# A fused block-sparse attention and squared-ReLU MLP kernel: mask and one-hot rows built another way, weights staged through eight buffers

## The chip, the cores and the metric

The kernel runs on one core of a Trainium2 chip. The metric is device time in microseconds (us) of one execution. It is the median over several executions; before the change three executions took 393.23, 394.69 and 397.41 us, so the median is 394.69 us. A core has five engines that run their own instruction streams and wait for one another through semaphores: PE (matrix products; PEld is its weight load), DVE (VectorE), ACT (ScalarE), POOL (GpSimd) and SP (SyncE, which in this kernel issues the DMA transfers).

## The reference

Four batches, eight heads, 768 positions, head size 64. Each query block of 32 positions may look at neighbouring blocks, at the first and last block, and at three sampled blocks. The attention output then goes through a two-layer MLP with a squared ReLU.

```
scores = scale * q @ k.T
mask   = |blk_i - blk_j| <= 1  or  either block is first or last  or  blk_j in sampled_blocks[blk_i]
attn   = softmax(where(mask, scores, -1e9))
x      = (attn @ v), heads joined          # 3072 tokens x 512
g      = relu(x @ w_in) ** 2               # w_in  512 x 2048
out    = g @ w_out                         # w_out 2048 x 512
```

Inputs and output are float32, the block list is 64-bit integers (the kernel reads the low 32-bit half). Matrix products run on bfloat16.

## The kernel before, in words

**Attention.** Heads go in pairs; a pair of one batch is a unit `u`, and there are 16 units, four to a batch. A unit has nine steps `s` (three stretches of 256 queries by three pairs of key chunks), 144 steps in all. `scores(s)` makes four products K·Q into the PSUM tile `ps`, and ACT takes the exponential into `pT`. `values(s - 2)` multiplies by V into `po`, of which there is one buffer, and every third step DVE copies `po` out into `et`.

**The mask.** It is not added by an engine: it rides in the products. The operands have extra rows under (QA, KA) or above (QB, KB) the 64 rows of data. In K these rows are a one-hot code of the key's block (24 rows); in Q they hold, for each query, 0 or a large negative number by block. The position order inside a tile is permuted: column n·128+p stands for position p·6+n. Before, DVE builds two 24-column tables (`oh`, `t2`), on all partitions, and `spread` (L146) writes each out to 24x768 in the permuted order, four tensors for each of two alternating buffer sets, eight copies in all.

**Loading and preparation.** `load(u)` issues three transfers (`qs`, `ks`, `vs`) on SP; `cast_qk` and `cast_v` turn them into bfloat16 on DVE; `transp` has PE transpose them and DVE copy the result into the data rows.

**After a unit.** `sums_out` sends the softmax sums from `et` into a small tile `st`, `recip` takes the reciprocal on DVE and sends it to DRAM (`rd`), `spread_recip` reads it back broadcast over 64 partitions (`rt`), and `normalize` multiplies `et` by it into `xT`.

**Weights.** There are 16 pieces of 512 KB. `w_load(i)` brings a piece into a float32 stage `wst`, `w_cast(i)` casts it on DVE into `w_in_sb` or `w_out_sb`.

**MLP.** For each batch, `h_atom` makes four products into `ph`, DVE takes the ReLU (`r`), POOL squares it (`g`), and `y_atom` makes four products into `py`. The pieces are spread evenly over 36 attention steps by the loop at the end, which starts a batch's MLP `LAG` steps after its last attention step; what is left of the last batch runs alone at the end.

**Order.** Each engine runs its instructions in the order in which the code emits them; nothing is reordered. `at(s, f)` puts `f` behind `scores(s)` and ahead of the MLP pieces and `values(s - 2)` of that step. Hence a DVE instruction that waits for a transfer also holds everything behind it on DVE, and an SP transfer that waits holds all later transfers. Each transfer also takes one of eight semaphores in turn, so a transfer waits until the one eight places ahead of it has landed.

Of the kernel before, what the change touches and what calls it, by code (L numbers as in the profile page):

```python
# [24 lines left out]
def kernel(  # L25
# [15 lines left out]
    nc = tc.nc  # L41
    B, H, S, D = q.shape
    block = 32
    nb = S // block
# [5 lines left out]
    NCH = S // P  # L50
# [37 lines left out]

    sb_i = consts.tile([P, nb * n_rand * 2], I32, name="sb_i")
    sb32 = sampled_blocks.bitcast(I32)  # L90
    nc.sync.dma_start(
        out=sb_i, in_=sb32.rearrange("q r -> (q r)").unsqueeze(0).broadcast_to([P, nb * n_rand * 2]))
    load(0)
    load(1)


    identb = consts.tile([P, P], BF, name="identb")
    make_identity(nc, identb)


    kbi = consts.tile([P, 1], I32, name="kbi")
    nc.gpsimd.iota(kbi[:64, :], pattern=[[0, 1]], base=0, channel_multiplier=1)
    nc.gpsimd.iota(kbi[64:, :], pattern=[[0, 1]], base=0, channel_multiplier=1)
    qbi = consts.tile([P, nb], I32, name="qbi")
    nc.gpsimd.iota(qbi, pattern=[[1, nb]], base=0, channel_multiplier=0)

    QA, QB, KA, KB, VA, VB = [], [], [], [], [], []
    NPB = 2
    for i in range(NPB):
# [7 lines left out]
    kbf = consts.tile([P, 1], F32, name="kbf")  # L117
    qbf = consts.tile([P, nb], F32, name="qbf")
    sbf = consts.tile([P, nb, n_rand], F32, name="sbf")
    eq = consts.tile([P, nb, n_rand], F32, name="eq")  # L120
    hit = consts.tile([P, nb], F32, name="hit")
    t1 = consts.tile([P, nb], F32, name="t1")
    t2 = consts.tile([P, nb], F32, name="t2")
    oh = consts.tile([P, nb], F32, name="oh")
    edge = consts.tile([P, 2], F32, name="edge")
    V = nc.vector
    V.tensor_copy(out=kbf, in_=kbi)
    V.tensor_copy(out=qbf, in_=qbi)

    V.tensor_scalar(out=oh, in0=qbf, scalar1=kbf, scalar2=None, op0=AOP.is_equal)  # L130
    V.tensor_scalar(out=t1, in0=qbf, scalar1=kbf, scalar2=None, op0=AOP.subtract)
    V.tensor_scalar(out=t2, in0=t1, scalar1=-1.0, scalar2=None, op0=AOP.is_ge)
    V.scalar_tensor_tensor(out=t1, in0=t1, scalar=1.0, in1=t2, op0=AOP.is_le, op1=AOP.mult)
    V.tensor_scalar(out=edge[:, 0:1], in0=kbf, scalar1=0.0, scalar2=None, op0=AOP.is_equal)
    V.tensor_scalar(out=edge[:, 1:2], in0=kbf, scalar1=float(nb - 1), scalar2=None, op0=AOP.is_equal)
    V.tensor_scalar(out=t1, in0=t1, scalar1=edge[:, 0:1], scalar2=edge[:, 1:2], op0=AOP.max, op1=AOP.max)
    V.memset(t1[:, 0:1], 1.0)
    V.memset(t1[:, nb - 1:nb], 1.0)
    sb_lo = sb_i.rearrange("p (q r two) -> p q r two", r=n_rand, two=2)[:, :, :, 0]
    V.tensor_copy(out=sbf, in_=sb_lo)  # L140
    V.tensor_scalar(out=eq, in0=sbf, scalar1=kbf, scalar2=None, op0=AOP.is_equal)
    V.tensor_reduce(out=hit, in_=eq, axis=AX.X, op=AOP.max)
    V.tensor_max(out=t2, in0=hit, in1=t1)
    V.tensor_scalar(out=t2, in0=t2, scalar1=-1.0, scalar2=-NEG, op0=AOP.add, op1=AOP.mult)

    def spread(dst, src, lo):  # L146

        V.tensor_copy(
            out=dst[lo:lo + nb, :].rearrange("k (n p) -> k p n", p=P),
            in_=src[lo:lo + nb, :].unsqueeze(2).broadcast_to([nb, nb, block]))  # L150

    G = nc.gpsimd
    for i in range(NPB):
        G.memset(QB[i][0:64, :], 0.0)
        G.memset(KB[i][0:64, :], 0.0)
        spread(KA[i], oh, 64)
        spread(KB[i], oh, 0)
        spread(QA[i], t2, 64)
        spread(QB[i], t2, 0)
        if i == 0:  # L160
            pass

    cast = {}

    def cast_qk(u):
        qs, ks, vs = raw[u]
        qc = work.tile([P, NCH, 2, D], BF, name="qc", tag="qc")
        kc = work.tile([P, NCH, 2, D], BF, name="kc", tag="kc")
        V.tensor_copy(out=qc, in_=qs.rearrange("p t n d -> p n t d"))  # L169
        V.tensor_copy(out=kc, in_=ks.rearrange("p t n d -> p n t d"))  # L170
        cast[u] = (qc, kc)

    def cast_v(u):
        vs = raw[u][2]
        i = u % NPB
        V.tensor_copy(out=VA[i][:, :, 0:D], in_=vs[:, 0])
        V.tensor_copy(out=VB[i][:, :, D:P], in_=vs[:, 1])

    def init_v(i):
        G.memset(VA[i][:, :, D:P], 0.0)  # L180
        G.memset(VA[i][:, :, D:D + 1], 1.0)
        G.memset(VB[i][:, :, 0:D], 0.0)
        G.memset(VB[i][:, :, 0:1], 1.0)

    def transp(u, which):
        src = cast[u][which]
        i = u % NPB
        A, Bt = (QA[i], QB[i]) if which == 0 else (KA[i], KB[i])
        pt = ps_h.tile([P, S], BF, name="pt", tag="h")
        for n in range(NCH):  # L190
            nc.tensor.transpose(pt[:, n * P:(n + 1) * P],  # L191
                                src[:, n, :, :].rearrange("p t d -> p (t d)"), identb)
        V.tensor_copy(out=A[0:D, :], in_=pt[0:D, :])  # L193
        V.tensor_copy(out=Bt[D:P, :], in_=pt[D:P, :])  # L194
# [86 lines left out]
    def recip(u):  # L281
        st = stile.pop(u)
        rc = work.tile([2 * SR, S // SR], F32, name="rc", tag="rc")
        V.reciprocal(out=rc, in_=st)  # L284
        rd = dram.tile([2, S], F32, name="rd", tag="rd")
        nc.sync.dma_start(out=rd.rearrange("t (a b) -> (t a) b", a=SR), in_=rc)
        rdram[u] = rd

    def spread_recip(u):
        rd = rdram.pop(u)  # L290
        rt = work.tile([P, S], F32, name="rt", tag="rt")
        nc.sync.dma_start(out=rt[0:D, :], in_=rd[0:1, :].broadcast_to([D, S]))
        nc.sync.dma_start(out=rt[D:P, :], in_=rd[1:2, :].broadcast_to([D, S]))
        rtile[u] = rt

    def normalize(u):
# [4 lines left out]
        V.tensor_mul(out=xT[b][0:D, a, :], in0=et[0:D, 0, :], in1=rt[0:D, :])  # L301
        V.tensor_mul(out=xT[b][D:P, a, :], in0=et[D:P, 1, :], in1=rt[D:P, :])  # L302
# [46 lines left out]
        return [z for _, _, z in sorted(both, key=lambda e: e[:2])]  # L349


    for i in range(NPB):
        init_v(i)
        if i == 0:
            cast_qk(0)
            cast_v(0)
    transp(0, 0)
    transp(0, 1)

    later = {}  # L360

    def at(s, f):
        later.setdefault(s, []).append(f)

    SPU = NQ * CP
    for u in range(NU):
        s0 = u * SPU
        if u + 2 < NU:
            at(s0 + 1, lambda u=u: load(u + 2))
# [68 lines left out]
```

## Time and profile before

| what | value |
|---|---|
| median of three executions | 394.69 us |
| the profiled execution, its own time | 392.2 us |
| its span, first to last instruction | 390.4 us |
| PE busy | 321.2 us (82%) |
| DVE busy | 238.2 us (61%) |
| ACT busy | 160.1 us (41%) |
| POOL busy | 113.8 us (29%) |
| moved by DMA | 40.49 MB, mean 104 GB/s |

The execution's own time is 1.8 us longer than the span. In the profile's rows, a line starts with the start time in us and the duration; in the stretch table each engine has its busy time; "PEclk" is the share of the full TensorE clock that was granted; a row of waits names the engine and line that waited, what it waited for, the total, the number and the longest. A DMA row on SP (SPq) is the issue of a transfer, not the transfer.

### The profile page before, as it was taken

Reading aid. Unit: us, or ns where it says so; the run is one execution under the profiler, and the core shown is the slowest. Engines: PE = TensorE matmul, PEld = TensorE weight load, DVE = VectorE, ACT = ScalarE, POOL = GpSimd, SP = SyncE. Lnnn points to the kernel's source line nnn. Section 1 sums busy time; section 2 is a strip of 40 time slices with the busy share of each in tenths; the row PEclk is TensorE's granted clock in tenths of the full one; section 3 lists DMA queues with packets and bytes.
Section 4 is the critical chain, followed back from the end, with each engine's and each line's share of the span. In section 5 each row is a group of like instructions: output and inputs, shape, how many; then the busy total and the mean of one; then the engine's idle time right before and its main releaser. Section 6 shows DMA issues by size and latency. Waiting matters only on the chain.

```text
span 390.4 us, 5784 instructions
## 1 busy us (share of the span) xinstructions
PE 321.2 (82%) x2215; PEld 217.7 (56%) x2240; DVE 238.2 (61%) x392; ACT 160.1 (41%) x169; POOL 113.8 (29%) x149
## 2 busy tenths in 40 slices
PE   0048627347889889999999999999999997999995
PEld 0037515235766666777667667666676663555542
DVE  7975625337677868677777667767665465444410
ACT  1027523236765545565554545554545521001011
POOL 5000000000004643233324343333433433666530
PEclk9999865688989999999999999999999999999999
DMA  7055356665550404421450155014111102000111
GB/s 234 15 160 191 110 156 229 208 202 177 164 161 19 146 19 146 128 93 41 151 188 31 40 152 190 31 53 156 49 60 37 41 30 95 29 27 28 55 54 54
DMA packets 23595, 40.49 MB, mean 104 GB/s; under 512 B 2960, under 2 KB 15376, under 8 KB 23568
## 3 DMA queue, kind: packets, MB, share of 16 engines
q1 hardware_dynamic: 23568, 40.13, 31.5%
q8 instruction: 17, 0.28, 0.3%
q14 instruction: 10, 0.08, 0.1%
HBM read 33.63 MB, written 6.39 MB: 102 GB/s over the span
## 4 chain that ended last, share of the span: by engine, by line
PE 62%; DVE 16%; DMA 14%; issue 3%; SPq 2%; ACT 1%; POOL 1%; DVEq 0%; ACTq 0%
PE py L325 19%; PE ph L310 17%; PE po L260 6%; PE po L262 6%; PE ps L244 6%; PE ps L242 6%; DMA st<-et 4%; DVE r L313 2%; DMA wst<-in_moe_w_in_dram 2%; DVE et L267 2%; PE pt L191 2%; DMA wst<-in_moe_w_out_dram 2%; DMA rd<-rc 2%; DMA sb_i<-in_sampled_blocks_dram 1%; DMA qs<-in_q_dram 1%
## 5 line engine op out<-in xcount | busy, mean ns | idle before, releaser
L246 ACT ACTIVATE pT<-ps 128x1024 bf16<-128x1024 f32 x144 | 145.8, 1023 | 161.8 <-PE ps L244 161.7
L315 POOL TENSOR_TENSOR g<-r 128x384 bf16<-128x384 f32 x128 | 108.0, 851 | 261.3 <-DVE r L313 261.3
L313 DVE TENSOR_SCALAR r<-ph 128x384 f32<-128x384 f32 x128 | 70.8, 556 | 71.1 <-PE ph L310 52.6
L310 PE MATMUL ph<-xT,w_in_sb 128*128 128x384 bf16 x512 | 100.9, 325 | 4.1 <-DVE r L313 3.4
L260 PE MATMUL po<-pT,VA 128*128 128x256 bf16 x288 | 75.5, 287 | 33.9 <-DVE et L267 33.9
L325 PE MATMUL py<-w_out_sb,g 128*128 128x512 bf16 x359 | 92.9, 379 | 3.1 <-ACT ys L329 1.4
L242 PE MATMUL ps<-QA,KA 88*128 88x256 bf16 x288 | 76.5, 288 | 1.4 <-DVE KA L193 1.2
L244 PE MATMUL ps<-QB,KB 128*128 128x256 bf16 x288 | 76.0, 286 | 0.3 <-DVE KB L194 0.3
L262 PE MATMUL po<-pT,VB 128*128 128x256 bf16 x288 | 75.7, 287 | 0.0
L310 PEld LDWEIGHTS <-w_in_sb 128*128 128x128 bf16 x512 | 49.5, 97 | 36.6 <-issue 3.8
L262 PEld LDWEIGHTS <-VB 128*128 128x128 bf16 x288 | 29.4, 102 | 48.5 <-issue 37.3
L325 PEld LDWEIGHTS <-g 128*128 128x128 bf16 x384 | 36.9, 97 | 35.0 <-issue 3.4
L329 ACT COPY ys<-py 128x512 f32<-128x512 f32 x24 | 14.0, 583 | 64.9 <-PE py L325 64.5
L267 DVE COPY et<-po 128x512 f32<-128x512 f32 x48 | 33.0, 688 | 11.4 <-PE po L262 10.9
L260 PEld LDWEIGHTS <-VA 128*128 128x128 bf16 x288 | 29.5, 103 | 11.8
L242 PEld LDWEIGHTS <-KA 88*128 88x128 bf16 x288 | 29.7, 103 | 6.7 <-DVE KA L193 1.4
L244 PEld LDWEIGHTS <-KB 128*128 128x128 bf16 x288 | 29.8, 103 | 6.2 <-issue 1.1
L191 PE MATMUL pt<-identb,qc 128*128 128x128 bf16 x96 | 8.6, 230 | 22.8 <-DVE qc L169 22.8
L284 DVE RECIPROCAL rc<-st 16x96 f32<-16x96 f32 x16 | 11.8, 737 | 17.2 <-DMA st<-et 17.2
L191 PEld LDWEIGHTS <-qc 128*128 128x128 bf16 x96 | 7.1, 103 | 23.3 <-DVE qc L169 22.8
L301 DVE TENSOR_TENSOR xT<-et,rt 64x768 bf16<-64x768 f32 x16 | 16.1, 1006 | 2.2 <-DMA rt<-rd 2.2
L302 DVE TENSOR_TENSOR xT<-et,rt 64x768 bf16<-64x768 f32 x16 | 15.3, 955 | 0.5
(48 smaller groups left out, 126.3 us busy)
## 6 DMA issues: line engine op xcount, KB each, us to landing
qs<-in_q_dram SPq DMA_DIRECT2D x16, 384.0 KB
ks<-in_k_dram SPq DMA_DIRECT2D x16, 384.0 KB
vs<-in_v_dram SPq DMA_DIRECT2D x16, 384.0 KB
rt<-rd SPq DMA_DIRECT2D x32, 192.0 KB
out_dram<-ys SPq DMA_DIRECT2D x24, 256.0 KB
wst<-in_moe_w_in_dram SPq DMA_DIRECT2D x8, 512.0 KB
wst<-in_moe_w_out_dram SPq DMA_DIRECT2D x8, 512.0 KB
st<-et SPq DMA_DIRECT2D x32, 3.0 KB
```

The source lines that it names most:

```text
L191: nc.tensor.transpose(pt[:, n * P:(n + 1) * P], src[:, n, :, :].rearrange("p t d -> p (t d)"), identb)
L242: nc.tensor.matmul(ps[:, c, 0, :], KA[i][0:64 + nb, ksl], QA[i][0:64 + nb, qsl], start=True, stop=True)
L244: nc.tensor.matmul(ps[:, c, 1, :], KB[i][:, ksl], QB[i][:, qsl], start=True, stop=True)
L246: nc.scalar.activation(out=pT, in_=ps, func=AF.Exp, scale=scale)
L260: nc.tensor.matmul(po[:, 0, :], VA[i][:, n, :], pT[:, c, 0, :], start=first, stop=last, skip_group_check=True)
L262: nc.tensor.matmul(po[:, 1, :], VB[i][:, n, :], pT[:, c, 1, :], start=False, stop=last, skip_group_check=True)
L267: V.tensor_copy(out=etile[u][:, :, qi * QW:(qi + 1) * QW], in_=po)
L301: V.tensor_mul(out=xT[b][0:D, a, :], in0=et[0:D, 0, :], in1=rt[0:D, :])
L310: nc.tensor.matmul(ph, w_in_sb[:, kc, f * P:(f + 1) * P], xT[b][:, kc, t * TW:(t + 1) * TW], start=(kc == 0), stop=(kc == KM - 1))
L313: V.tensor_scalar(out=r, in0=ph, scalar1=0.0, scalar2=None, op0=AOP.max)
L315: G.tensor_mul(out=g, in0=r, in1=r)
L325: nc.tensor.matmul(py, gtile[b, t, f][:, ts * P:(ts + 1) * P], w_out_sb[:, f, :], start=(f == 0), stop=(f == NF - 1))
```

## The change

1. **Mask and one-hot rows.** POOL makes the one-hot rows of K directly in the permuted order: DVE sets the 64x768 area to one, and two selects (`affine_select`) on POOL clear what lies outside the block. The table of masks is worked out by DVE on 24 partitions, in a PSUM tile `pm`, and goes as a 24x128 bfloat16 tile `bm` into two small products with the one-hot rows (`pb`); ACT copies the result into the rows of Q. The block list comes in as 24x6 integers, not broadcast to 128 partitions. Only the first buffer set is made in this way; the second is copied from it by four transfers on SP.
2. **Start.** `ks` of the first unit is issued by ACT; the first casts and transposes stand ahead of `init_v` and `cast_v`.
3. **Weights.** `wst` has eight buffers where it had two. `w_load(i)` stands at step 2+2i (before: 9+i) and `w_cast(i)` at 10+2i (before: 12+i).
4. **After a unit.** `recip` and `spread_recip` stand one step later, `normalize` two, and `LAG` is 12, not 10.

```diff
-    def load(u):
+    def load(u, eng):
...
-        nc.sync.dma_start(out=ks.rearrange("p t n d -> p t (n d)"), in_=kv[b, a])
+        eng.dma_start(out=ks.rearrange("p t n d -> p t (n d)"), in_=kv[b, a])
...
-    sb_i = consts.tile([P, nb * n_rand * 2], I32, name="sb_i")
...
+    sb_i = consts.tile([nb, n_rand * 2], I32, name="sb_i")
+    nc.sync.dma_start(out=sb_i, in_=sampled_blocks.bitcast(I32))
+    load(0, nc.scalar)
+    load(1, nc.sync)
...
+    G.iota(rel, pattern=[[1, nb]], base=0, channel_multiplier=-1, **small)
+    G.iota(col, pattern=[[1, nb]], base=0, channel_multiplier=0, **small)
+    G.iota(row, pattern=[[0, 1]], base=0, channel_multiplier=1, **small)
+    def one_hot(dst):
+        d3 = dst.rearrange("a (n p) -> a n p", p=P)
+        G.affine_select(out=d3, in_=d3, compare_op=AOP.is_ge, fill=0.0, base=0,
+                        pattern=[[1, NCH], [NCH, P]], channel_multiplier=-block)
+        G.affine_select(out=d3, in_=d3, compare_op=AOP.is_ge, fill=0.0, base=block - 1,
+                        pattern=[[-1, NCH], [-NCH, P]], channel_multiplier=block)
+    V.memset(KB[0][0:64, :], 1.0)
+    V.memset(KA[0][64:P, :], 1.0)
+    one_hot(KB[0][0:64, :])
+    identb = consts.tile([P, P], BF, name="identb")
+    make_identity(nc, identb)
+    one_hot(KA[0][64:P, :])
...
-    def spread(dst, src, lo):
-        V.tensor_copy(
-            out=dst[lo:lo + nb, :].rearrange("k (n p) -> k p n", p=P),
-            in_=src[lo:lo + nb, :].unsqueeze(2).broadcast_to([nb, nb, block]))
-    for i in range(NPB):
-        G.memset(QB[i][0:64, :], 0.0)
-        G.memset(KB[i][0:64, :], 0.0)
-        spread(KA[i], oh, 64)
-        spread(KB[i], oh, 0)
-        spread(QA[i], t2, 64)
-        spread(QB[i], t2, 0)
...
+    pm = ps_h.tile([nb, 4, nb], F32, name="pm", tag="h")
...
+    for lo in (0, 64):
+        V.tensor_scalar(out=bm[:, lo:lo + nb], in0=pm[:, cur, :], scalar1=-1.0, scalar2=-NEG,
+                        op0=AOP.add, op1=AOP.mult)
+    pb = ps_s.tile([P, 1024], F32, name="pb", tag="ps")
+    nc.tensor.matmul(pb[:, 0:512], bm, KB[0][0:nb, 0:512], start=True, stop=True)
+    nc.tensor.matmul(pb[:, 512:S], bm, KB[0][0:nb, 512:S], start=True, stop=True)
+    nc.scalar.copy(out=QB[0][0:64, :], in_=pb[0:64, 0:S])
+    nc.scalar.copy(out=QA[0][64:P, :], in_=pb[64:P, 0:S])
...
-        st = ld.tile([P, 1024], F32, name="wst", tag="wst")
+        st = ld.tile([P, 1024], F32, name="wst", tag="wst", bufs=8)
...
-    for i in range(NPB):
-        init_v(i)
-        if i == 0:
-            cast_qk(0)
-            cast_v(0)
+    cast_qk(0)
     transp(0, 0)
     transp(0, 1)
+    init_v(0)
+    cast_v(0)
+    for i in range(1, NPB):
+        nc.sync.dma_start(out=KA[i][64:P, :], in_=KA[0][64:P, :])
+        nc.sync.dma_start(out=KB[i][0:64, :], in_=KB[0][0:64, :])
+        nc.sync.dma_start(out=QA[i][64:P, :], in_=QA[0][64:P, :])
+        nc.sync.dma_start(out=QB[i][0:64, :], in_=QB[0][0:64, :])
+        init_v(i)
...
-        at(e + 2, lambda u=u: recip(u))
-        at(e + 2, lambda u=u: spread_recip(u))
-        at(e + 6, lambda u=u: normalize(u))
+        at(e + 3, lambda u=u: recip(u))
+        at(e + 3, lambda u=u: spread_recip(u))
+        at(e + 8, lambda u=u: normalize(u))
     for i in range(2 * NWP):
-        at(9 + 2 * i // 2, lambda i=i: w_load(i))
-        at(12 + 2 * i // 2, lambda i=i: w_cast(i))
+        at(2 + 2 * i, lambda i=i: w_load(i))
+        at(10 + 2 * i, lambda i=i: w_cast(i))
...
-    LAG = 10
+    LAG = 12
```

Three places show how the instructions move. First, DVE in the stretch between the third copy-out `et` of the first unit and its `normalize` (tile `xT`), before the change (`wst` are the staged weight pieces, `pt` the transposed data, `rc` the reciprocals):

```order
L267 COPY et_254<-po_309 128x2x256
L218 CAST w_in_sb_153<-wst_321 128x1024
L284 RECIPROCAL rc_389<-st_358 16x96
L193 COPY QA0_104<-pt_396 64x768
L194 COPY QB0_105<-pt_396 64x768
L218 CAST w_in_sb_153<-wst_344 128x1024
L267 COPY et_412<-po_363 128x2x256
L176 CAST VA0_108<-vs_203 128x6x64
L177 CAST VB0_109<-vs_203 128x6x64
L218 CAST w_in_sb_153<-wst_361 128x1024
L193 COPY KA0_106<-pt_438 64x768
L194 COPY KB0_107<-pt_438 64x768
```

The same stretch on DVE after the change, from the same copy-out on:

```order
L265 COPY et_255<-po_314 128x2x256
L216 CAST w_in_sb_146<-wst_249 128x1024
L191 COPY QA0_94<-pt_391 64x768
L192 COPY QB0_95<-pt_391 64x768
L265 COPY et_404<-po_365 128x2x256
L282 RECIPROCAL rc_413<-st_362 16x96
L174 CAST VA0_98<-vs_200 128x6x64
L175 CAST VB0_99<-vs_200 128x6x64
L216 CAST w_in_sb_146<-wst_287 128x1024
L191 COPY KA0_96<-pt_437 64x768
L192 COPY KB0_97<-pt_437 64x768
```

Three more instructions, among them a copy-out of `po`, now stand between the unit's last copy-out and the reciprocal that waits for the transfer `st`, and the copies of the transposed Q no longer stand behind that wait.

Second, SP at the start, one piece of the difference, from the four copies of the second buffer set on (KA_96 is the first set's KA, KA_102 the second's):

```order
+L357 DMA KA_102<-KA_96 64x768
+L358 DMA KB_103<-KB_97 64x768
+L359 DMA QA_100<-QA_94 64x768
+L360 DMA QB_101<-QB_95 64x768
 L84 DMA qs<-in_q_dram 128x2x384
 L85 DMA ks<-in_k_dram 128x2x384
 L86 DMA vs<-in_v_dram 128x2x384
-L208 DMA wst<-in_moe_w_in_dram 128x1024
+L206 DMA wst<-in_moe_w_in_dram 128x1024 x4
```

The four copies stand ahead of the third unit's load, and four weight pieces follow that load, where one followed it before.

Third, SP around the first unit's sums (`st`, `rd`, `rt`), up to the next unit's load, before the change:

```order
L277 DMA st<-et 8x1x96
L278 DMA st<-et 8x1x96
L208 DMA wst<-in_moe_w_in_dram 128x1024 x2
L286 DMA rd<-rc 16x96
L292 DMA rt<-rd 64x768
L293 DMA rt<-rd 64x768
L208 DMA wst<-in_moe_w_in_dram 128x1024 x4
L211 DMA wst<-in_moe_w_out_dram 128x2x512 x2
L84 DMA qs<-in_q_dram 128x2x384
```

The same place after the change:

```order
L275 DMA st<-et 8x1x96
L276 DMA st<-et 8x1x96
L206 DMA wst<-in_moe_w_in_dram 128x1024
L284 DMA rd<-rc 16x96
L290 DMA rt<-rd 64x768
L291 DMA rt<-rd 64x768
L206 DMA wst<-in_moe_w_in_dram 128x1024 x2
L209 DMA wst<-in_moe_w_out_dram 128x2x512
L84 DMA qs<-in_q_dram 128x2x384
```

One piece instead of two now stands between the sums and the reciprocals' transfer, and three instead of six between the broadcast and the next unit's load.

More of the change, by code (lines that the diff above doesn't have):

```diff
@@ L84, in load @@
         nc.sync.dma_start(out=qs.rearrange("p t n d -> p t (n d)"), in_=qv[b, a])
-        nc.sync.dma_start(out=ks.rearrange("p t n d -> p t (n d)"), in_=kv[b, a])
+        eng.dma_start(out=ks.rearrange("p t n d -> p t (n d)"), in_=kv[b, a])
         nc.sync.dma_start(out=vs.rearrange("p t n d -> p t (n d)"), in_=vv[b, a])
         raw[u] = (qs, ks, vs)
-    sb_i = consts.tile([P, nb * n_rand * 2], I32, name="sb_i")
[L90 to L105, printed above, removed]
+    sb_i = consts.tile([nb, n_rand * 2], I32, name="sb_i")
+    nc.sync.dma_start(out=sb_i, in_=sampled_blocks.bitcast(I32))
+    load(0, nc.scalar)
+    load(1, nc.sync)
+    V, G = nc.vector, nc.gpsimd
     QA, QB, KA, KB, VA, VB = [], [], [], [], [], []
@@ L115 @@
         VB.append(consts.tile([P, NCH, P], BF, name=f"VB{i}"))
[L117 to L142, printed above, removed]
@@ L143 @@
[L143 to L161 removed]
+    rel = consts.tile([nb, nb], F32, name="rel")
@@ new lines @@
+    col = consts.tile([nb, nb], F32, name="col")
+    row = consts.tile([nb, 1], F32, name="row")
+    small = dict(allow_small_or_imprecise_dtypes=True)
+    G.iota(rel, pattern=[[1, nb]], base=0, channel_multiplier=-1, **small)
[7 more added lines that the diff above has]
+                        pattern=[[-1, NCH], [-NCH, P]], channel_multiplier=block)
@@ new lines @@
+    V.memset(KB[0][0:64, :], 1.0)
[4 more added lines that the diff above has]
+    one_hot(KA[0][64:P, :])
+    bm = consts.tile([nb, P], BF, name="bm")
+    sbf = consts.tile([nb, n_rand], F32, name="sbf")
+    edge = consts.tile([nb, 2], F32, name="edge")
+    V.memset(bm, 0.0)
+    pm = ps_h.tile([nb, 4, nb], F32, name="pm", tag="h")
+    V.tensor_scalar(out=pm[:, 0, :], in0=rel, scalar1=-1.0, scalar2=None, op0=AOP.is_ge)
@@ new lines @@
+    V.scalar_tensor_tensor(out=pm[:, 1, :], in0=rel, scalar=1.0, in1=pm[:, 0, :],
+                           op0=AOP.is_le, op1=AOP.mult)
+    V.tensor_scalar(out=edge[:, 0:1], in0=row, scalar1=0.0, scalar2=None, op0=AOP.is_equal)
+    V.tensor_scalar(out=edge[:, 1:2], in0=row, scalar1=float(nb - 1), scalar2=None, op0=AOP.is_equal)
+    V.tensor_scalar(out=pm[:, 0, :], in0=pm[:, 1, :], scalar1=edge[:, 0:1], scalar2=edge[:, 1:2],
+                    op0=AOP.max, op1=AOP.max)
+    V.memset(pm[:, 0, 0:1], 1.0)
@@ new lines @@
+    V.memset(pm[:, 0, nb - 1:nb], 1.0)
+    V.tensor_copy(out=sbf, in_=sb_i.rearrange("q (r two) -> q r two", two=2)[:, :, 0])
+    cur = 0
+    for r in range(n_rand):
+        V.scalar_tensor_tensor(out=pm[:, 1 - cur, :], in0=col, scalar=sbf[:, r:r + 1],
+                               in1=pm[:, cur, :], op0=AOP.is_equal, op1=AOP.max)
+        cur = 1 - cur
+    for lo in (0, 64):
+        V.tensor_scalar(out=bm[:, lo:lo + nb], in0=pm[:, cur, :], scalar1=-1.0, scalar2=-NEG,
+                        op0=AOP.add, op1=AOP.mult)
@@ L368 @@
         if u + 2 < NU:
-            at(s0 + 1, lambda u=u: load(u + 2))
+            at(s0 + 1, lambda u=u: load(u + 2, nc.sync))
         if u + 1 < NU:
```

1 line of the change is left out of this document (removed).

## The prediction

> **What bounds the kernel now.** I read the page first.
>
> ```profile
> span 390.4 us, 5784 instructions
> PE   0048627347889889999999999999999997999995
> PEclk9999865688989999999999999999999999999999
> ```
>
> A slice is 9.8 us. PE is idle in the first two slices, half used up to the twelfth and full from then on. So the kernel has three parts: a start, a stretch of attention without MLP, and a long part that PE sets. The table by stretches, cut at the first score product and where the pace changes, gives sizes:
>
> ```profile
> core 0: us, PE busy (x) PEld busy (x) DVE busy (x) ACT busy (x) POOL busy (x), PEclk, DMA share, GB/s
> 0.00:25.39 25.39, 1.46 (x12) 1.20 (x12) 22.39 (x32) 1.28 (x1) 5.75 (x21) 1.00 0.34 114
> 25.39:43.30 17.91, 15.55 (x126) 12.29 (x127) 8.61 (x17) 13.71 (x14) 0.00 (x0) 1.00 0.54 173
> 43.30:94.19 50.89, 25.50 (x149) 18.82 (x149) 25.73 (x43) 16.16 (x16) 0.00 (x0) 0.70 0.63 204
> 94.19:116.77 22.58, 17.71 (x153) 14.47 (x151) 14.96 (x26) 15.59 (x16) 0.00 (x0) 0.92 0.45 141
> 150.00:200.00 50.00, 49.52 (x375) 35.37 (x378) 37.38 (x61) 28.76 (x31) 16.76 (x19) 1.00 0.29 98
> ```
>
> DVE fills the start (22.39 of 25.39 us). In 43.30 to 94.19 only 16 steps pass (ACT x16) in 50.89 us, and no engine is busy for more than 26. The later part has PE at 49.52 of 50. The timeline shows what DVE does in the start, and the first product:
>
> ```profile
> 7.31 1.87 DVE L148 CAST KA<-oh 24x768 bf16<-24x768 f32 x1
> ...
> 20.46 1.86 DVE L148 CAST QB<-t 24x768 bf16<-24x768 f32 x1
> 21.94 0.76 DVE L169 CAST qc<-qs 128x768 bf16<-128x768 f32 x1
> ...
> 25.39 0.40 PE L242 MATMUL ps<-QA,KA 88*128 88x256 bf16 x1 [1.18 <-DVE KA L193]
> ```
>
> Eight spreads in a row, then the first cast; 3.45 us from that cast to the first product. Waits between 25.4 and 116.8 us name the slow stretch:
>
> ```profile
> PE po L260 <- DVE et L267: 32.1, 13, 7.1
> DVE rc L284 <- DMA st<-et: 13.1, 4, 5.8
> DVE w_in_sb L218 <- DMA wst<-in_moe_w_in_dram: 9.2, 3, 6.8
> DVE w_out_sb L221 <- DMA wst<-in_moe_w_out_dram: 6.3, 3, 4.4
> ```
>
> DVE waits for transfers (28.6 us together), the copy-out `et` is queued behind those waits, and PE waits 32.1 us for it. The MLP begins here:
>
> ```profile
> 116.61 0.81 PE L310 MATMUL ph<-xT,w_in_sb 128*128 128x384 bf16 x4
> ```
>
> The attention stretch is thus 116.61 - 25.39 = 91.2 us for 46 steps.
>
> **The start, part by part.** The eight spreads go (15 us of DVE) and so do the small operations on the 72-column list. New prices have no row of their own; the nearest:
>
> ```profile
> 1.01 0.29 POOL masks.py:199 TENSOR_SCALAR_AFFINE_SELECT identb<-identb 128x128 bf16<-128x128 bf16 x1
> 2.40 0.76 POOL L155 MEMSET KB<- 64x768 bf16 x1
> 3.25 0.67 DVE L132 TENSOR_SCALAR t<-t 128x24 f32<-128x24 f32 x1
> 3.96 0.18 DVE L133 SCALAR_TENSOR_TENSOR t<-t,t 128x24 f32<-128x24 f32 x1
> 0.74 4.77 DMA sb_i<-in_sampled_blocks_dram
> ```
>
> A select of 768 columns lies between 0.76 us (a fill of that tile) and six times 0.29, 1.74 us. I take 1.74, since it is the same operation. POOL: three iotas to about 1.3, two selects to 4.8, identity 0.5, two selects to 8.8 us. DVE: two fills of up to 0.76 to about 2.2; eight small operations at 0.18 to 0.67, say 2.2 in all, to 4.4; the block list, which is smaller now and lands no later than 5.51 (0.74 + 4.77); six more operations, 1.2, to 6.7. The transfers of `qs` and `ks`:
>
> ```profile
> 2.00:3.00 1.00, 0.00 (x0) 0.00 (x0) 0.96 (x3) 0.01 (x1) 1.00 (x2) 1.00 0.49 67
> 3.00:4.00 1.00, 0.00 (x0) 0.00 (x0) 0.93 (x4) 0.00 (x0) 1.00 (x3) 1.00 0.60 129
> 4.00:5.00 1.00, 0.00 (x0) 0.00 (x0) 0.67 (x6) 0.00 (x0) 0.99 (x2) 1.00 0.80 283
> 5.00:6.00 1.00, 0.00 (x0) 0.00 (x0) 0.47 (x1) 0.00 (x0) 0.90 (x4) 1.00 1.06 391
> ```
>
> 0.87 MB had moved by 6.0 us and the two take 0.79 MB, so they are there by about 6 to 6.5. The cast starts at 6.8, the first product 3.45 later, at 10.3 us. The mask branch ends beside it: `bm` at 6.7, two products (under 1 us), two ACT copies of 768 columns, at most the 1.02 us of the 1024-column exponential quoted below, 10 us. POOL's 8.8 is earlier still. `init_v` falls behind 8.8 on POOL and is covered, since `cast_v` is first needed two steps on. The four bias copies hold SP until about 10 us and land by 13, and unit 1 needs them at step 9, some 20 us; I cost them at nothing; without that cover, up to 3 us. `ks` on ACT costs one issue on an engine that is idle there. **Gain: 25.39 - 10.3 = 15.1 us.** Ends: 8.5 us (cast at 5) to 15 (selects at 3.4).
>
> The Trainium skill, "SBUF — State Buffer", section "Who interferes with whom", says that a DVE copy or cast in its fast mode and a POOL operation block each other for a whole instruction. The pair above agrees: 0.67 us while POOL fills, 0.18 for a like operation. By that rule the casts of q and k could each stand behind a running select, an estimate of 3.5 us more, and the sum below would be 356.5 instead of 353.
>
> **The attention stretch.** 48 steps now (`LAG` 12). The pace without congestion, and the waits and casts that matter:
>
> ```profile
> 26.91 1.94 ACT L246 ACTIVATE pT<-ps 128x1024 bf16<-128x1024 f32 x2 [24.89 <-PE ps L244]
> ...
> 43.30 1.02 ACT L246 ACTIVATE pT<-ps 128x1024 bf16<-128x1024 f32 x1 [0.16 <-PE ps L244]
> ```
>
> ```profile
> 68.22 0.69 DVE L221 CAST w_out_sb<-wst 128x1024 bf16<-128x1024 f32 x1 [1.32 <-DMA wst<-in_moe_w_out_dram]
> 74.76 0.74 DVE L284 RECIPROCAL rc<-st 16x96 f32<-16x96 f32 x1 [5.85 <-DMA st<-et]
> 95.60 0.74 DVE L284 RECIPROCAL rc<-st 16x96 f32<-16x96 f32 x1 [2.61 <-DMA st<-et]
> ```
>
> Thirteen steps in 16.39 us are 1.26 a step, with one wait for `st` in them. Steps 0 to 9 have no reciprocal: 1.2 each, 12 us. Steps 10 to 39 carry the sixteen casts. DVE without casts has 14.96 us in 16 steps, 0.935 a step; a cast of 0.69 every second step adds 0.345: 1.28, above ACT's 1.02, so DVE sets the pace and its waits come on top. The wait for `st` was 2.61 with a quiet queue and 5.85 with loads ahead of it; one step later it is shorter by about 1.4, so 1.2 to 4.4, middle 2.8; three in thirty steps, 0.28 a step. Together 1.56: 46.8 us. Steps 40 to 47: 22.58 us for 16 steps with two waits of 2.6 are 1.41; without the waits 1.08; I take 1.25: 10 us. The waits for `wst` (15.5 us) go: a piece has eight steps and eight buffers, so its transfer starts about 10 us before its cast. Sum 12 + 46.8 + 10 = 69 us. **Gain: 91.2 - 69 = 22.2 us.**
>
> **The rest.** Two attention steps have left PE's long part. In the chain of waits, PE starts a product of 256 columns every 0.21 us in its first steps and every 0.11 us at full clock:
>
> ```profile
> 28.36 0.21 PE ps L244
> ...
> 30.06 0.11 PE ps L242
> ```
>
> Two steps of eight products are 1.8 us. At the end of attention the last normalisation stalls DVE and then PE:
>
> ```profile
> 329.33 0.95 DVE L301 TENSOR_TENSOR xT<-et,rt 64x768 bf16<-64x768 f32 x1 [2.21 <-DMA rt<-rd]
> ...
> 331.91 0.81 PE L310 MATMUL ph<-xT,w_in_sb 128*128 128x384 bf16 x4 [2.43 <-DVE r L313]
> ```
>
> Two more steps of MLP stand ahead of it now, at over 1 us each, so these 2.4 us go; nothing to 2.4. **Sum:** 15.1 + 22.2 + 1.8 + 2.4 = 41.5 us off the profiled execution's 392.2 us: 350.7. The median of the runs lies 2.5 above that execution; with it, 353 us.
>
> **The rivals.** *The pace of ACT.* If the waits for `st` fall beside other work, 48 steps at 1.26 are 60.5 us; 344.7 us. For it: the 14 steps before the slow stretch ran so; against it: DVE has 1.28 a step of work of its own. *Transfers set the pace.* The sizes:
>
> ```profile
> qs<-in_q_dram SPq DMA_DIRECT2D x16, 384.0 KB
> ...
> rt<-rd SPq DMA_DIRECT2D x32, 192.0 KB
> ...
> wst<-in_moe_w_in_dram SPq DMA_DIRECT2D x8, 512.0 KB
> ```
>
> Five units (15 x 384 KB), 16 pieces, eight broadcasts and the bias copies are 16.2 MB. At the 204 GB/s of the slow stretch that is 79 us from 11 us on, MLP at some 92, 366 us. Against it: 391 GB/s moved at the start, and in the slow stretch the transfer engines were busy only 63% of the time. *The selects cost more than I think* (the part does not do what it says): at 5 us each the first product is at 22, and the time 364. *PE at half clock through the stretch:* products every 0.21 us, 1.86 us a step with the transposes, 89 us, 373.5. The granted 0.70 of the slow stretch speaks for it; the 1.00 of 25.39 to 43.30, where PE was busy 87%, against. The Trainium skill, "TensorE: Matmul & The Clock Gate", section "What's actually happening", has the gate halve the clock after an idle window of about 3.4 us; by that only a wait for `st` longer than that would bring it, and the trace agrees that the half clock lies in the stretch with the long waits. *Slower:* the read-ahead stands ahead of `st`. Four weight pieces and a load (3.3 MB) at 204 GB/s are 16 us, four times over steps 11 to 41, with DVE, and so PE, held each time: 53 us more than my four waits of 2.8, 406 us. It decides from about 14 us a wait; the longest seen is 5.85, and the order puts three pieces and a load ahead of a unit's sums (more ahead of the first unit's, but issued some 8 us earlier).
>
> **How the numbers follow.** Forecast (346 to 360) 0.48; ACT's pace 0.18; transfers 0.17; selects 0.06; half clock 0.06; slower 0.03; no visible effect, the gains eaten by several of these, 0.02. The range 340 to 368 takes in the forecast, most of ACT's pace, transfers and selects, about 0.84. Executions of before differ by 1%, which is about what tells a change from none. Faster by over 1%: 0.95; within 1%: 0.02; slower: 0.03.
>
> **What would show it.** First score product at 9 to 12 us; no row of waits of DVE for `wst` above 2 us in all; four waits of `rc` for `st` of 1 to 4.5 us; MLP's first product near 80 us with DVE above 80% busy between steps 10 and 40; granted clock above 0.9 there; no PE idle ahead of the last batch. A first product after 16 us, a stretch with the transfers at their best rate throughout, or waits of `st` beyond 8 us would prove it wrong.

## The result, and the profile after

The changed kernel takes 367.12 us in the median (366.48 to 368.65, four executions), against 394.49 us before (393.23 to 397.41, four executions). The ratio is 0.930, 95% interval 0.924 to 0.936. The profiled execution took 366.48 us, with a span of 364.8 us. That is 14 us above the forecast of 353 us, outside the forecast's own band (346 to 360), just inside the range (340 to 368), and at the time that the rival "transfers set the pace" gave (366).

The page of the changed kernel, span and slices (9.1 us each):

```profile
span 364.8 us, 5787 instructions
PE   2896637675979898989999999999999998999995
PEclk9999997999999999999999999999999999999999
```

PE now works from the second slice on, and the clock is down in one slice where it was down in seven. The table by stretches, cut at the same events as before (first score product, first MLP product):

```profile
core 0: us, PE busy (x) PEld busy (x) DVE busy (x) ACT busy (x) POOL busy (x), PEclk, DMA share, GB/s
0.00:8.74 8.74, 2.21 (x14) 1.35 (x15) 6.26 (x22) 2.87 (x3) 6.96 (x20) 1.00 0.78 263
8.74:86.56 77.82, 52.76 (x441) 42.70 (x441) 50.92 (x88) 47.07 (x48) 0.27 (x2) 0.96 0.70 226
86.56:364.80 278.24, 260.64 (x1763) 169.21 (x1787) 161.30 (x275) 110.97 (x120) 111.91 (x128) 1.00 0.24 75
```

For before, the third row by the same cuts is this one:

```profile
116.61:390.40 273.79, 261.10 (x1781) 171.00 (x1803) 166.62 (x278) 113.52 (x123) 108.03 (x128) 1.00 0.23 76
```

So three terms moved: the start from 25.39 to 8.74 us (16.7 gained), the attention stretch, from the first score product to the first MLP product, from 91.2 to 77.8 us (13.4 gained), and the long part from 273.8 to 278.2 us (4.4 lost), though PE has the same work in it less two attention steps. Waits in the stretch of the changed kernel:

```profile
PE po L258 <- DVE et L265: 24.7, 15, 6.3
DVE QA L191 <- PE pt L189: 12.7, 5, 3.9
DVE xT L299 <- DMA rt<-rd: 7.3, 4, 3.9
DVE rc L282 <- DMA st<-et: 0.8, 1, 0.8
```

No row names a weight stage `wst` any more. The wait for the sums `st` has almost gone too, and a wait for the broadcast `rt` has come in its place. In the long part of the changed kernel, and of the kernel before, PE's wait for copy-outs is:

```profile
PE po L258 <- DVE et L265: 6.6, 9, 1.5
```

```profile
PE po L260 <- DVE et L267: 1.9, 2, 1.7
```

In the long part of the changed kernel the timeline shows what stands on DVE around a normalisation (`xT`); the last number in brackets is idle time ahead of an instruction:

```profile
99.63 0.56 DVE L311 TENSOR_SCALAR r<-ph 128x384 f32<-128x384 f32 x1 [0.97 <-POOL g L313]
100.11 0.94 DVE L299 TENSOR_TENSOR xT<-et,rt 64x768 bf16<-64x768 f32 x1
101.08 1.47 DVE L300 TENSOR_TENSOR xT<-et,rt 64x768 bf16<-64x768 f32 x1
102.58 0.56 DVE L167 CAST qc<-qs 128x768 bf16<-128x768 f32 x1
103.06 0.55 DVE L168 CAST kc<-ks 128x768 bf16<-128x768 f32 x1
103.53 1.01 DVE L311 TENSOR_SCALAR r<-ph 128x384 f32<-128x384 f32 x2
104.13 0.81 PE L308 MATMUL ph<-xT,w_in_sb 128*128 128x384 bf16 x4 [1.54 <-DVE r L311]
104.46 0.68 DVE L265 COPY et<-po 128x512 f32<-128x512 f32 x1
...
105.19 0.27 PE L258 MATMUL po<-pT,VA 128*128 128x256 bf16 x1 [0.25 <-DVE et L265]
```

For 3.4 us, 100.11 to 103.53, DVE does nothing for PE's running work: two normalisations, then the next unit's two casts. PE runs out of free `ph` buffers, waits 1.54 us, and then waits for the copy-out `et`. Here s0 is the first step of a unit and e = s0 + 11 (`e = s0 + SPU + 2` in the code). At e + 8 the normalisation falls on step s0 + 1 of a later unit, which has the casts and a copy-out already; at e + 6 it fell two steps ahead of them. Of the twelve normalisations that stand beside MLP, nine share the step with both, since the last units have no later unit whose q and k are to be cast; the row of 6.6 us above has nine waits, one at each of these.

### The profile page after: what moved, and what is told of

Its sections match the earlier page's. It is cut to its first block, busy times and chain, and to the rows that moved or that the text cites. A ratio compares the mean times of both kernels' runs of the same rounds, so it can differ in the third digit from the quotient of the medians.

```text
span 364.8 us, 5787 instructions
## 1 busy us (share of the span) xinstructions
PE 315.6 (87%) x2215; PEld 213.3 (58%) x2242; DVE 218.5 (60%) x384; ACT 160.9 (44%) x171; POOL 119.1 (33%) x149
## 4 chain that ended last, share of the span: by engine, by line
PE 62%; DVE 21%; DMA 9%; issue 4%; ACT 1%; SPq 1%; POOL 1%; DVEq 0%; ACTq 0%
PE py L323 19%; PE ph L308 18%; PE po L258 6%; PE ps L242 5%; PE po L260 5%; PE ps L240 5%; DMA rt<-rd 4%; DVE et L265 4%; DVE xT L300 4%; DVE r L311 3%; DVE xT L299 2%; DMA rd<-rc 2%; PE pt L189 2%; DVE qc L167 2%; DVE kc L168 2%
## 5 line engine op out<-in xcount | busy, mean ns | idle before, releaser
L313 POOL TENSOR_TENSOR g<-r 128x384 bf16<-128x384 f32 x128 | 111.9, 881 | 229.3 <-DVE r L311 229.1
L258 PE MATMUL po<-pT,VA 128*128 128x256 bf16 x288 | 71.9, 276 | 31.3 <-DVE et L265 31.3
L240 PE MATMUL ps<-QA,KA 88*128 88x256 bf16 x288 | 74.0, 280 | 1.5 <-DVE KA L191 1.3
L242 PE MATMUL ps<-QB,KB 128*128 128x256 bf16 x288 | 73.8, 280 | 0.1
L260 PE MATMUL po<-pT,VB 128*128 128x256 bf16 x288 | 72.0, 276 | 0.0
L260 PEld LDWEIGHTS <-VB 128*128 128x128 bf16 x288 | 28.4, 99 | 46.1 <-issue 36.2
L258 PEld LDWEIGHTS <-VA 128*128 128x128 bf16 x288 | 28.4, 99 | 10.9
L191 DVE COPY QA<-pt 64x768 bf16<-64x768 bf16 x16 | 8.8, 550 | 24.6 <-PE pt L189 24.6
L300 DVE TENSOR_TENSOR xT<-et,rt 64x768 bf16<-64x768 f32 x16 | 21.0, 1314 | 1.1 <-DMA rt<-rd 0.7
L299 DVE TENSOR_TENSOR xT<-et,rt 64x768 bf16<-64x768 f32 x16 | 15.7, 984 | 7.4 <-DMA rt<-rd 7.3
L191 DVE COPY KA<-pt 64x768 bf16<-64x768 bf16 x16 | 8.8, 547 | 3.6 <-PE pt L189 3.5
```

The lines of the kernel that those rows point to most:

```text
L240: nc.tensor.matmul(ps[:, c, 0, :], KA[i][0:64 + nb, ksl], QA[i][0:64 + nb, qsl], start=True, stop=True)
L242: nc.tensor.matmul(ps[:, c, 1, :], KB[i][:, ksl], QB[i][:, qsl], start=True, stop=True)
L258: nc.tensor.matmul(po[:, 0, :], VA[i][:, n, :], pT[:, c, 0, :], start=first, stop=last, skip_group_check=True)
L260: nc.tensor.matmul(po[:, 1, :], VB[i][:, n, :], pT[:, c, 1, :], start=False, stop=last, skip_group_check=True)
L313: G.tensor_mul(out=g, in0=r, in1=r)
```

## The experiments

All runs are on one core, beside runs of the kernel before on the same chip. The kernel before took 392.5 to 394.5 us in them, so times from different runs compare to within some 2 us. Theory A: the place e + 8 crowds one step on DVE and PE waits. Theory B: the long part lost for another reason (`LAG`, or POOL's squares holding up the normalisation wherever it is). Theory C: transfers set the pace of the stretch.

**One step earlier, one step later.** The same kernel with the normalisation moved.

```diff
-        at(e + 8, lambda u=u: normalize(u))
+        at(e + 7, lambda u=u: normalize(u))     # norm7; norm9: e + 9
```

> The changed kernel with normalize one step earlier (e + 7, not e + 8), nothing else. Theory A, the crowded step: at e + 8 the normalisation falls on the step in which DVE also has the two casts of the next unit and a copy-out of po, some 3.7 us of DVE in one step, and PE waits for the copy-out. A expects the waits of PE for et after the MLP has begun to fall from 9.8 us to 3 us or less and the time to fall from 367 to about 358 to 362 us. Theory B, the long part is slower for another reason (LAG 12, or POOL's squares that hold up the normalisation wherever it stands): 365 to 368 us, the waits for et stay near 9 us. Theory C, the broadcast rt lands late behind weight pieces: the wait for rt in the first 87 us grows from 8 to some 12 us and eats 3 to 4 us of any gain.

> The changed kernel with normalize one step later (e + 9), behind the copy-out of po of that crowded step, nothing else. A expects much the same as at e + 7: waits of PE for et after the start of the MLP at 3 us or less, 357 to 362 us. B expects 365 to 369 us. C expects it to be better than e + 7 by the wait for rt in the first stretch, 3 to 6 us.

At e + 7: 359.76 us (ratio 0.916, 0.912 to 0.921). At e + 9: 354.96 us (0.904, 0.901 to 0.907). Both neighbours of e + 8 are faster, by 7 and 12 us, so lateness or earliness as such is not the cause. The long parts of e + 7 and e + 9:

```profile
86.03:358.20 272.17, 259.90 (x1763) 169.35 (x1787) 166.47 (x275) 111.08 (x120) 110.83 (x128) 1.00 0.23 77
```

```profile
81.88:353.00 271.12, 259.87 (x1763) 169.38 (x1787) 165.43 (x276) 111.08 (x120) 107.49 (x128) 1.00 0.24 79
```

278.2 us have become 272.2 and 271.1 with the same PE work. In the timeline at e + 9 the block is split, and the ReLU `r` and the copy-out stand between its halves:

```profile
96.02 0.55 DVE L167 CAST qc<-qs 128x768 bf16<-128x768 f32 x1
96.49 1.19 DVE L168 CAST kc<-ks 128x768 bf16<-128x768 f32 x1
97.60 1.01 DVE L311 TENSOR_SCALAR r<-ph 128x384 f32<-128x384 f32 x2
98.53 0.68 DVE L265 COPY et<-po 128x512 f32<-128x512 f32 x1
99.13 1.52 DVE L299 TENSOR_TENSOR xT<-et,rt 64x768 bf16<-64x768 f32 x1
100.67 0.96 DVE L300 TENSOR_TENSOR xT<-et,rt 64x768 bf16<-64x768 f32 x1
```

PE's wait for copy-outs in the long part falls from 6.6 us to 2.0 at e + 7, and at e + 9 no row of it is left; A had expected 3 us or less. A's times were 358 to 362 and 357 to 362 us; e + 9 did better than that, because its stretch fell too, from 77.8 to 72.7 us:

```profile
9.15:81.88 72.73, 56.42 (x440) 44.49 (x441) 49.70 (x88) 47.30 (x48) 0.00 (x0) 0.91 0.68 235
```

C's part is half borne out: the wait for `rt` in the stretch is 0.6 us at e + 9 and 6.9 us at e + 7, so the later place saves it, but at e + 7 it did not grow to 12 us as expected.

**The fourth part undone, and one number of it put back.** First all four places as before the change (e + 2, e + 6, `LAG` 10) with start and weights as changed; then the same with e + 8 alone.

```diff
-        at(e + 3, lambda u=u: recip(u))           # and spread_recip
-        at(e + 8, lambda u=u: normalize(u))
-    LAG = 12
+        at(e + 2, lambda u=u: recip(u))           # and spread_recip
+        at(e + 6, lambda u=u: normalize(u))       # old_norm8: e + 8
+    LAG = 10
```

> The changed kernel with the old places behind a unit: recip at e + 2, normalize at e + 6, LAG 10; start and weights as changed. This measures the fourth part of the change alone. The prediction held that part to gain some 4 us (end of attention, wait for st): that would give about 371 us. A expects the long part back at 274 us and the wait for st back at 5 to 10 us: 360 to 366 us. B, if LAG is the cause: 358 to 362 us.

> The changed kernel with the old places behind a unit (recip e + 2, LAG 10: 357.1 us), but normalize at e + 8. One number differs from that run. Theory A: the step s0 + 1 is crowded again, the long part (first MLP product to the end) grows from 273 us by 5 to 10 us, 363 us or more. If LAG or the place of the reciprocal had made the changed kernel slow: 355 to 359 us.

The old places take 357.11 us (0.909, 0.906 to 0.912): on top of the other parts, the fourth costs 10 us, where the prediction had it gain. Both expectations for this run (360 to 366 and 358 to 362 us) were too high. With e + 8 put back the time is 372.12 us (0.948, 0.942 to 0.954), 15 us more from one number. The two long parts, old places first:

```profile
82.34:355.30 272.96, 262.54 (x1781) 171.51 (x1803) 166.71 (x279) 113.64 (x123) 108.24 (x128) 0.99 0.23 77
```

```profile
81.26:369.40 288.14, 265.31 (x1806) 171.38 (x1803) 164.96 (x279) 113.53 (x123) 112.52 (x128) 0.99 0.22 73
```

The whole loss lies in the long part (15.2 us); the stretches are 73.6 and 72.1 us. That is more than the 5 to 10 us expected, and not all of it is the crowded step. PE's wait for copy-outs in the long part is 0.2 us with the old places and this with e + 8:

```profile
PE po L258 <- DVE et L265: 9.5, 9, 1.9
```

And with `LAG` 10 a batch's MLP begins in the very step of that normalisation: the row "PE ph <- DVE xT" has 6.0 us in three waits, and the old places have no such row. These two make up the loss to within a microsecond or two. B's `LAG` falls as the cause: the step is slow with `LAG` 10 and e + 9 is fast with 12. That POOL's squares hold up the normalisation is true, but the price was paid before too, on another instruction (last section). Between this run and the changed kernel (372 against 367) the later reciprocal and `LAG` 12 give some 5 us back; which of the two was not tried.

**The parts alone.** The start alone (parts 1 and 2 of the change), and the weights alone (part 3, put into the kernel before).

> Only the start as changed (mask rows, one-hot rows, order of the first casts); weights through two buffers and all places as in the kernel before. The first product came 16.7 us earlier with the whole change (8.74 against 25.39 us). If the parts add up: 394.5 - 16.7 = 378 us, the attention stretch still 91 us long. If the slow stretch is set by the amount of data to be moved, which starts earlier now but at the same rate, the same 378 us; if the stretch gets longer because the loads no longer have 16 idle us ahead of them, 381 to 388 us.

> The kernel before with only the third part of the change: eight stage buffers, loads at 2 + 2i, casts at 10 + 2i; the old start and the old places behind a unit. With the start as changed and the old places, the weights part alone took 376.5 down to 357.1 us, 19.4 us. If it does not need the earlier start: 393.2 - 19.4 = 374 us, the attention stretch at 74 us. If it needs the idle transfer time of an early start: 378 to 385 us; if the long start gives it more time to read ahead: 368 to 372 us.

The start alone takes 376.49 us (0.959, 0.955 to 0.962), 16.7 us less than before, exactly what the first product came earlier. The weights alone take 372.52 us (0.952, 0.946 to 0.959), 20.4 us less; on top of the changed start they are worth 19.4 us (376.49 to 357.11). So the two parts add and neither needs the other. The steps -16.7 - 19.4 + 10 make -26 us, against 27 measured; they add up by their making, since each run continues the one before, and the fourth part was not run alone. The stretch with the weights part alone, and with the start alone:

```profile
24.69:97.98 73.29, 53.28 (x425) 42.71 (x426) 48.49 (x83) 44.96 (x46) 0.00 (x0) 0.93 0.68 228
```

```profile
8.74:101.15 92.41, 60.01 (x425) 46.39 (x426) 49.58 (x85) 45.23 (x46) 0.28 (x2) 0.78 0.59 192
```

**Are transfers the pace?** Half of each weight piece is loaded and that half cast twice; the other half of the weights is left out.

```diff
-            nc.sync.dma_start(out=st, in_=wiv[:, kc, hf * 1024:(hf + 1) * 1024])
+            nc.sync.dma_start(out=st[:, 0:512], in_=wiv[:, kc, hf * 1024:hf * 1024 + 512])   # w_out likewise
...
-            V.tensor_copy(out=w_in_sb[:, kc, hf * 1024:(hf + 1) * 1024], in_=st)
+            V.tensor_copy(out=w_in_sb[:, kc, ...].rearrange("p (t d) -> p t d", t=2),
+                          in_=st[:, 0:512].unsqueeze(1).broadcast_to([P, 2, 512]))   # w_out_sb likewise
```

> The changed kernel with half of each weight piece loaded (256 KB, not 512 KB) and that half cast twice, so that DVE has the same number of elements; the weights are therefore wrong and the rest of the work is the same. 4.2 MB less are moved in the attention stretch. Theory C, transfers set the pace of the stretch: it falls from 77.8 us by 10 to 18 us, the time to 350 to 357 us, the waits for rt and st (8.8 us) go. Theory A, the crowded step on DVE and PE sets it: the waits of DVE for rt go, the stretch falls by 3 to 8 us, the time to 359 to 364 us, and the waits of PE for et stay above 15 us.

365.01 us (0.930, 0.925 to 0.935): the ratio to the kernel before is that of the changed kernel. The stretch:

```profile
9.15:83.88 74.73, 55.29 (x440) 44.26 (x441) 50.74 (x88) 47.23 (x48) 0.00 (x0) 0.91 0.55 177
```

4.2 MB less take 3.1 us off it, not 10 to 18. C falls as the bound of the stretch, though the median lies a little above what A expected; the wait for `rt` went to 3.9 us, not to nothing.

**The queue that the weights stand in.** From e + 9, the weight transfers issued by ACT.

```diff
-            nc.sync.dma_start(out=st, in_=wiv[:, kc, hf * 1024:(hf + 1) * 1024])
+            nc.scalar.dma_start(out=st, in_=wiv[:, kc, hf * 1024:(hf + 1) * 1024])   # w_out likewise
```

> normalize at e + 9 (355.0 us), and the 16 weight transfers issued by ACT at their own steps, so that none stands ahead of st, rd or rt on SP. If the sums wait behind the weight pieces on SP's queue (waits of rc for st 6.8 us in the stretch): those waits fall below 3 us and the time to 350 to 353 us. If the transfers share the same engines whatever queue they stand in: no change, 354 to 357 us; the issues on ACT (16 of some 0.5 us) may cost up to 3 us of the stretch.

352.53 us (0.900, 0.895 to 0.905); the interval overlaps that of e + 9. The wait for `st` in the stretch fell from 6.8 to 2.5 us, as expected of a wait in the queue, and the wait for `rt` rose from 0.6 to 2.5 us. Some gain is likely and its size open.

**Is DVE's own work the pace?** From e + 9, the weight casts on POOL.

```diff
-            V.tensor_copy(out=w_in_sb[...], in_=st)
+            G.tensor_copy(out=w_in_sb[...], in_=st)          # w_out_sb likewise
```

> normalize at e + 9 (355.0 us), and the sixteen casts of the weights on POOL, which is idle in the attention stretch, not on DVE: 11 us of DVE leave the stretch. The prediction's step, DVE's own work of 1.28 us a step sets the pace between steps 10 and 39: the stretch falls from 72.7 us by 7 to 11 us, 344 to 348 us. If the pace is set by DVE and PE waiting for each other in turn (copy-outs, transposes), and the casts lie in the gaps: it falls by 0 to 4 us, 351 to 355 us. If POOL holds up DVE's own casts and copies while it casts: 355 us or more.

351.49 us (0.894, 0.890 to 0.898). Stretch and waits of that run:

```profile
9.14:77.46 68.32, 52.66 (x441) 42.55 (x441) 42.04 (x72) 47.07 (x48) 17.97 (x16) 0.95 0.75 247
```

```profile
PE po L258 <- DVE et L265: 15.3, 14, 4.0
DVE rc L282 <- DMA st<-et: 8.2, 3, 4.1
```

DVE has 7.7 us less work in the stretch (49.7 to 42.0) and the stretch is 4.4 us shorter (72.7 to 68.3). PE still waits 15.3 us for copy-outs (15.9 at e + 9) and DVE 8.2 us for sums. So DVE's work is likely a part of the pace, and not the whole. How large a part is open, since the granted clock in the stretch also differs, 0.91 at e + 9 and 0.95 here, and PE is busy for 3.8 us less.

**Two smaller moves**, from e + 9: the casts of q and k at s0 + 3, not s0 + 1; and the reciprocal with its broadcast at e + 4, not e + 3.

> normalize at e + 9 and the casts of the next unit's q and k two steps later (s0 + 3, not s0 + 1), so that no DVE work of a unit's end shares a step with a copy-out. Theory A, carried on: the remaining waits of PE for et in the stretch (15.9 us) fall further, 349 to 353 us. If the casts at s0 + 1 cost nothing any more, since the copy-out behind them is only 1.1 us late: 354 to 356 us. If the transposes one step later now come late for the next unit: 357 us or more.

> normalize at e + 9 (355.0 us), and recip and the broadcast one step later (e + 4). The wait of rc for st in the stretch (6.8 us) should fall to 2 us or less; rt has five steps instead of six, so the wait for rt may grow from 0.6 to 3 us. If a wait removed on DVE is a wait saved: 350 to 353 us. If DVE then waits somewhere else (rt, transposes): 354 to 357 us.

The later casts cost 5 us: 359.93 us (0.917, 0.911 to 0.923). In the stretch PE now waits for them: the row "PE pt <- DVE qc" has 3.6 us, and e + 9 has no such row. But the stretch is only 0.8 us longer (73.6 us), since the waits for copy-outs fell too, from 15.9 to 12.6 us. The rest of the loss lies in the long part:

```profile
82.72:358.00 275.28, 261.35 (x1763) 169.48 (x1787) 165.75 (x278) 111.06 (x120) 108.96 (x128) 1.00 0.24 77
```

Against 271.1 us at e + 9 that is 4.2 us; PE waits there 3.1 us for ReLUs (1.2 at e + 9) and 1.1 for the casts, and no row accounts for the rest. Spreading DVE's work is no good in itself; it has to stand where nobody waits. The later reciprocal takes 353.56 us (0.899, 0.894 to 0.904), which overlaps e + 9: the wait for `st` fell to 4.8 us, not to 2 as expected, and that for `rt` rose to 2.4.

**All together.** e + 9, weights issued by ACT and cast by POOL, reciprocal at e + 4.

> normalize at e + 9 together with the three small edits: weight transfers issued by ACT (gave 2.4 us), weight casts on POOL (3.5 us), recip at e + 4 (1.4 us). If the gains add: 355.0 - 7.3 = 347.7 us, the stretch near 65 to 67 us. If they all take away the same waits of DVE for st and rt: 350 to 352 us. The long part, which none of them touches, stays at 270 to 272 us in both.

348.76 us (0.890, 0.886 to 0.894), the lowest median of the runs, 18 us below the changed kernel. That is near the 347.7 us of gains that add, but the interval overlaps that of the casts on POOL alone (0.890 to 0.898), so it is not shown that they do. Its stretch:

```profile
9.16:75.52 66.36, 52.98 (x441) 42.77 (x442) 43.00 (x71) 47.01 (x48) 17.86 (x16) 0.95 0.78 251
```

66.4 us for 48 steps, with PE busy for 53.0 of them, ACT for 47.0 and DVE for 43.0. PE still waits 9.2 us for copy-outs there, and DVE 4.9 us for `rt`; what holds the rest is open.

## Why the prediction was right or wrong

**The start was right, its prices too high.** Forecast 10.3 us, measured 8.74. The timeline of the changed kernel:

```profile
1.80 0.86 POOL L118 TENSOR_SCALAR_AFFINE_SELECT KB<-KB 64x768 bf16<-64x768 bf16 x1 [0.57 <-DVE KB L123]
...
4.95 0.26 DVE L152 TENSOR_SCALAR bm<-pm 24x24 bf16<-24x24 f32 x2
...
5.08 1.79 POOL L120 TENSOR_SCALAR_AFFINE_SELECT KA<-KA 64x768 bf16<-64x768 bf16 x1
5.14 0.54 DVE L167 CAST qc<-qs 128x768 bf16<-128x768 f32 x1
...
8.74 0.37 PE L240 MATMUL ps<-QA,KA 88*128 88x256 bf16 x1 [1.27 <-DVE KA L191]
```

A select took 0.86 us, near the lower end (0.76) and not the 1.74 that I took; that is three times the 0.29 us of the 128-column select, for six times the columns. The mask table was done at 5.2 us, not 6.7, and the cast began at 5.14, not 6.8, with `qs` there by then and not at 6 to 6.5. From there to the first product it took 3.6 us (3.45 forecast). The gain of 16.7 us reached the end whole, as the start alone shows. The rival on the selects is out. The estimate of 3.5 us for casts that stand behind a running select was too high as well: the casts lost nothing here, and at e + 9 the first product came 0.4 us later (last section). The pair of rows beside that estimate (0.67 and 0.18 us) does not show the price, for POOL was filling during the 0.18 too (L155, 3.84 to 4.60 us). The operation of the 0.67, with POOL idle, is this row of the kernel before:

```profile
7.10 0.18 DVE L144 TENSOR_SCALAR t<-t 128x24 f32<-128x24 f32 x1
```

**The weights were right.** No wait for `wst` is left, and the weights part is worth 19 to 20 us. In the stretch the forecast was 69 us, measured 77.8 (8.8 too few): steps 0 to 9 took 13.4 us (12 forecast), 10 to 39 49.9 (46.8), 40 to 47 13.2 (10), each taken between the starts of ACT's exponentials. The step "three waits for `st` of 2.8 us" had the size of the waits nearly right, 8.4 us, but by luck, for the transfer was wrong: 0.8 us for `st`, 8.0 for `rt`. The reciprocal's transfer `rd` stood behind weight pieces on SP's queue and took 4.02 us, so the broadcast came late. I had looked at one end of that chain only. The step "DVE has 1.28 a step, so it sets the pace" failed, as the row of the changed kernel for steps 10 to 39 shows:

```profile
23.49:73.40 49.91, 31.89 (x281) 26.30 (x279) 34.09 (x57) 29.30 (x32) 0.00 (x0) 0.93 0.69 227
```

DVE was busy for 34.09 of 49.91 us, 68% and not over 80, and with 7.7 us of work taken off DVE at e + 9 the stretch was 4.4 us shorter. PE waits for copy-outs and DVE for transposes in turn; the model of one engine's sum does not see that. The place e + 9 takes 5.1 of the missing 8.8 us back.

**The rest was wrong, and is the term that failed in kind.** I had 4.2 us gained: two steps fewer in PE's long part and the stall at the end of attention gone. The stall did shrink, from 2.43 to 0.98 us. But the long part grew by 4.4 us, 8.6 us more than forecast. The sum had priced the moved normalisation at its last occurrence only. It has sixteen, twelve of them beside MLP, and for nine of these the step that it moved to held two casts and a copy-out. The move was not costed by what it now stands beside. At e + 9 the long part is 271.1 us, 1.5 us from the forecast of 269.6.

**The rivals.** "Transfers set the pace" gave the measured time by accident: half the weight bytes changed nothing. "Half clock" is out (granted 0.96 in the stretch), as is "slower" (waits for `st` 0.8 us in all, the longest wait of DVE for a transfer 3.91). ACT's pace was not reached, and its 1.26 us a step was miscounted: the table of before has fourteen steps (ACT x14) in those 16.39 us, not thirteen, so 1.17 a step and some 340 us for that rival; the combined kernel, at 66.4 us for 48 steps, is at 1.38.

## What to carry to other kernels

A step moved to a later place to give a transfer more time has to be costed in every repetition against what stands in its new place on the same engine; here two neighbouring places differed by 12 us of 367. The two normalisation products and the two casts took DVE no longer at e + 8 than at e + 9 (54.4 and 57.5 us in all, last section); what cost here was that they stood as one unbroken block ahead of a copy-out, not their sum. When a wait for one transfer is shortened, follow the chain to the next transfer (`st`, `rd`, `rt`), since the wait may only move along it.

## What the runs showed of the hardware that was not expected

**POOL and DVE hold each other up, at a price per instruction.** In the start of the changed kernel the last select took 1.79 us while DVE cast beside it, 0.86 otherwise (rows above): POOL paid and DVE did not, its cast took 0.54. At e + 9, with the same code in the start, it was the other way round:

```profile
5.09 0.86 POOL L120 TENSOR_SCALAR_AFFINE_SELECT KA<-KA 64x768 bf16<-64x768 bf16 x1
5.21 1.17 DVE L167 CAST qc<-qs 128x768 bf16<-128x768 f32 x1
```

The cast took 1.17 us there, and the first product came at 9.15 us, not 8.74. In the long part, the groups of the second product of the normalisation, before, changed kernel, and e + 8 with the old places:

```profile
L302 DVE TENSOR_TENSOR xT<-et,rt 64x768 bf16<-64x768 f32 x16 | 15.3, 955 | 0.5
```

```profile
L300 DVE TENSOR_TENSOR xT<-et,rt 64x768 bf16<-64x768 f32 x16 | 21.0, 1314 | 1.1 <-DMA rt<-rd 0.7
```

```profile
L300 DVE TENSOR_TENSOR xT<-et,rt 64x768 bf16<-64x768 f32 x16 | 21.5, 1343 | 0.5
```

The same product takes 0.96 us in the mean or 1.31 to 1.34, by what POOL does beside it (in the block shown above a square `g` runs on POOL from 100.27 to 101.73 us; it takes 1.46 us there and 0.83 just before, so POOL pays too). The Trainium skill, "SBUF — State Buffer", section "Who interferes with whom", says so of a two-input DVE operation beside a POOL operation that reads; the trace agrees, with 0.36 us here, 5.7 us over the sixteen. In the start the same section would have had either of the two wait, and it was POOL in the one run and DVE in the other; by the profile the select began first in both, by 0.06 and 0.12 us. The 5.7 us are no new loss, though, for the second cast of the next unit paid as much in the kernel before (first row) and nothing in the changed one:

```profile
L170 DVE CAST kc<-ks 128x768 bf16<-128x768 f32 x16 | 14.5, 906 | 0.0
L168 DVE CAST kc<-ks 128x768 bf16<-128x768 f32 x16 | 8.8, 553 | 1.1 <-DMA ks<-in_k_dram 1.1
```

The two products and the two casts together take DVE 55.0 us before, 54.4 in the changed kernel and 57.5 at e + 9, which is the faster. So the price moved to another instruction, and does not explain the longer long part.

**A small transfer behind large ones in its queue.** `rd` is 6 KB. It landed in 1.34 us with the queue quiet and in 4.02 us behind two weight pieces, which were issued from 39.15 us on, by the chains of waits of before and of the changed kernel:

```profile
96.37 1.34 DMA rd<-rc
```

```profile
44.19 4.02 DMA rd<-rc
```
